# Pooled attention in front of a SiLU layer: the 72 keys of a head split into 64 and 8, in smaller array tiles

## The chip, the cores and the metric

The kernel runs on one core of one Trainium2 chip. The metric is the device time of one execution in microseconds (us). PE is the matmul engine, DVE the vector engine, ACT the scalar engine, POOL the GpSimd engine, and SP an engine that here only issues transfers.

## The reference

```python
k_p = k.reshape(B, H, 72, 8, D).mean(axis=3)        # B = 8, H = 8, S = 576, D = 64
v_p = v.reshape(B, H, 72, 8, D).mean(axis=3)
scores = np.matmul(q, k_p.transpose(0, 1, 3, 2)) / np.sqrt(D)
attn = np.exp(scores - max); attn = attn / (sum + 1e-09)
x = (attn @ v_p) -> [4608 tokens, 512]
h = x @ w_in                                        # [512, 2048]
out = (h * sigmoid(h)) @ w_out                      # [2048, 512]
```

Each query of a head sees 72 pooled keys. All heads of a token side by side make the 512 inputs of the layer behind.

## The kernel before, in words

**Tiles and steps.** The 4608 tokens are taken in NT = 9 tiles of 512 (a tile can hold tokens of two batches, since a batch has 576; in units of 32 tokens, tile t takes 2t units of batch t-1 and 16-2t of batch t). Tile 0's attention is made first, in a piece of its own. After that the loop over t makes the two products of the layer for tile t, and beside them, in the same queue of PE, the attention of tile a = t+1. The products are made with sums of blocks (seven products of half size in place of eight): `x_sum` and `w_sum` are sums of blocks of the input and the weights, `h_sum` of the hidden values. They are DVE's work (lines 479, 474, 579, 590).

An order written by hand, such as `FOUR` for t from 2 to 7 or `FIRST` for t = 0, gives the sequence of products. `a1 a5 b1 ...` are units of the first product (two steps each of two matmuls of 256 columns); `P1 Q1 ... P4 Q4` are the first and second half of products of the second (four steps of two matmuls each). `at(s, fn, ...)` and `late(s, fn, ...)` place other work behind step s. The order in each engine's queue is the order in which this code runs: no scheduler moves anything later. In `FOUR`, step 63 is the end of unit d4, in front of P2; steps 68 to 75 are P5 and Q5 (they load `h_sum0`), 76 to 83 P6 and Q6 (`h_sum1`), 84 to 87 Q2, 88 to 91 P7.

**Banks.** PSUM has eight banks here: three under the tag `mm` and five under the tag `at`. The products use `mm` for `u_psB`, `o_psA`, `o_psB` and `o_psE`, and `at` for `u_psA` and `u_psE`. Attention takes its banks from `at` for the most part. A new tile of a tag gets the bank that was given back first.

**Attention of one tile (a >= 1).** PE can be cut into smaller arrays ("lanes") that work beside each other, each on its own rows and columns. The tile is made in two halves of 256 queries (f = 0, 1), in three visits to PE:

- step 63, `scores(a, 0)` and step 78, `scores(a, 1)`: `score_matmuls` (line 331) multiplies `kz` (keys, transposed, 32 rows for half of a head's dimensions) by `qT`. Lanes of 32 rows and 128 columns; four heads s in four lanes, c = 0, 1 the two halves of the dimensions, g = 0, 1 the two groups of four heads. Results are four banks `sc_ps` of 72 keys x 512; ACT makes `es`, their exponentials (line 356).
- step 89, `denominators` (line 363, `ones` times `es`), `numerators` (line 378, `vp`, the pooled values, times `es`) for both halves. Lanes of 128 rows (72 used) and 32 columns, four at once. ACT makes logarithm and exponential of the denominators (lines 368 and 373: `lnd`, `rec`), and `x_half` (line 413, DVE) multiplies `nu_ps` by `rec` into `xT`, from which the `x_sum`s of the next tile are made.

**Keys and values.** For batches 3 and up POOL loads k and v in two halves that are added in transfer (`load_one`, `load_rest`), adds the rest up (`pool_rows`, lines 189 and 192), and PE transposes the keys (`k_transpose`, step 34), ACT copying them into `kz` (line 213). Batches 0 to 2 go another way: rows are summed (`slot_sums`, line 261: DVE, in part POOL) and PE picks the rows of each head (`select_k`, line 283; `select_v`, line 301), ACT copying the result (`copy_v`, line 308).

Of the kernel before, what the change touches and what calls it, by code (L numbers as in the profile page):

```python
# [36 lines left out]
def kernel(  # L37
# [62 lines left out]
    ones = singles.tile([SP, 32], BF16, name="ones")  # L100
# [18 lines left out]
    kz = [singles.tile([128, 2, 2, SP], BF16, name=f"kz{n}") for n in range(2)]  # L119
    kp = singles.tile([128, H, D], BF16, name="kp")  # L120
# [44 lines left out]
    PH = POOL // 2 * D  # L165

# [9 lines left out]
    def load_one(b, name):  # L176
        st = batches.setdefault(b, {})
        raw = raw_tile(f"{name}_raw3", H)
        nc.gpsimd.dma_start(out=raw, in_=source(b, name)[:, :, :PH])
        st[f"{name}_raw"] = raw  # L180

    def load_rest(b, name):
        nc.gpsimd.dma_start(
            out=batches[b][f"{name}_raw"], in_=source(b, name)[:, :, PH:],
            accum_op=ALU.add,
        )
# [9 lines left out]

    def pool_v(b):
        st = batches[b]
        st["vp"] = mid.tile([SP, H, D], BF16, tag="vp", name="vp")
        pool_rows(st["vp"], st["v_raw"])  # L200
# [91 lines left out]
    def select_v(b, a, tag="at"):  # L292
        st = batches[b]
        if a == 0:
            st["v_ps"] = ps_tile([128, H, D], FP32, tag, "v_ps")
            st["vp"] = mid.tile([SP, H, D], BF16, tag="vp", name="vp")
# [8 lines left out]

    def copy_v(b, a, copy=nc.vector.tensor_copy, heads=4):
        hs = slice(4 * a, 4 * a + heads)
        copy(out=batches[b]["vp"][:, hs, :], in_=batches[b]["v_ps"][:SP, hs, :])
# [14 lines left out]
    def es_tile():  # L323
        return mid.tile([SP, 4, 2 * NQ], BF16, tag="es", name="es")
# [25 lines left out]
    def scores(t, f):  # L350
        sc = [ps_tile([128, 512], FP32, "at", "sc_ps")[:SP] for s in range(4)]
        for g in range(2):
            score_matmuls(sc, t, f, g, g * NQ)
        es = half_state(t, f)["es"] = es_tile()
        for s in range(4):
            nc.scalar.activation(es[:, s, :], sc[s], func=AF.Exp, scale=score_scale)  # L356

    def denominators(t, f, den_ps=None):
# [3 lines left out]
        for s in range(4):  # L362
            nc.tensor.matmul(  # L363
                den_ps[32 * s : 32 * (s + 1), :],
                lhsT=ones, rhs=st["es"][:, s, :], start=True, stop=True,
# [9 lines left out]
    def numerator_matmuls(nu, t, f, g, c, c0):  # L375
        for b, _, cs in half_units(t, f):
            for s in range(4):
                nc.tensor.matmul(  # L378
                    nu[32 * s : 32 * (s + 1), c0 + cs.start : c0 + cs.stop],
                    lhsT=batches[b]["vp"][:, 4 * g + s, c::2],  # L380
# [20 lines left out]
    def numerators(t, f, tags=("at", "at")):  # L401
        st = half_state(t, f)
        nu = []
        for c in range(2):
            nu.append(ps_tile([128, 512], FP32, tags[c], "nu_ps"))
            for g in range(2):
                numerator_matmuls(nu[c], t, f, g, c, g * NQ)
        st["nu"] = nu

    def x_half(t, f):  # L410
        st = half_state(t, f)
        for c in range(2):
            nc.vector.tensor_mul(  # L413
                out=xT[:, c::2, x_cols(t, f)],
                in0=st["nu"][c].rearrange("r (g n) -> r g n", g=2),
                in1=st["rec"].rearrange("r (g n) -> r g n", g=2),
# [364 lines left out]
    nc.vector.memset(kp, 0.0)  # L781
    nc.gpsimd.memset(shifts, 0.0)
    make_identity(nc, ident, nomemset=True)

# [76 lines left out]
    for n in range(4):  # L861
        unit_weight_sum(0, 1, n)
    denominators(0, 1, den_ps)
# [28 lines left out]
    for t in range(NT):  # L892
        a = t + 1
        if t == 0:
# [17 lines left out]
            for j in range(2):  # L912
                at(60 + 2 * j, select_k, 1, j)
                at(60 + 2 * j, copy_k, 1, j, nc.scalar.copy)
            for i0, i1 in ((0, SA), (SA, SLOTS), (SLOTS, SLOTS + 1)):
# [9 lines left out]
            for j in range(2):  # L925
                at(83 + j, slot_sums, "v", j)
                at(100 + j, select_v, 1, j)
            at(101, copy_v, 1, 0, nc.scalar.copy, H)
# [5 lines left out]
            at(68, scores, 1, 0)  # L934
            at(79, scores, 1, 1)
            at(79, denominators, 1, 0)
            at(94, reciprocals, 1, 0)
            at(103, denominators, 1, 1)
            at(103, reciprocals, 1, 1)
            at(106, numerators, 1, 0)  # L940
            at(106, numerators, 1, 1, ("at", "mm"))
# [107 lines left out]
```

## Time and profile before

| | |
|---|---|
| median of 3 runs | 273.23 us (273.04 to 273.35) |
| span of the profiled execution (first to last instruction) | 272.3 us |
| median less that span | 0.9 us |
| mean granted clock of PE | 0.999 |
| busy: PE, DVE, ACT, POOL | 266.3, 206.5, 194.1, 102.3 us |

The profiled execution has no time of its own beside its span; the 0.9 us is what lies around the span in the median run. In a line of the timeline the columns are the start in us from the span's start, the length of the group in us, the engine, the line of the kernel, the operation, what is written and read, shape and number of instructions. Matmuls overlap, so a group's length reaches beyond the start of the next group. In `128*128` or `72*32` the first number is rows, the second columns of the array in use.

### The profile page before, as it was taken

The page shows a single profiled execution, that of the slowest core. Times are in us where ns is not written, and L with a number is a line of the kernel's source. Part 1 is how long each engine was busy: PE and PEld are TensorE (multiplying, and loading weights), DVE is VectorE, ACT ScalarE, POOL GpSimd, SP SyncE. Part 2 cuts the span into 40 slices and gives each one's busy share as a digit, 9 for nine tenths or more (in the row PEclk, how much of TensorE's full clock was granted, in tenths as well). Part 3 has the DMA queues.
Part 4 walks back from the last instruction along what each step waited for, and adds up shares of the span by engine and source line. Part 5 has one row for each costly group of instructions (what it writes and reads, how often), then busy time and mean ns, then how long its engine had stood idle before and what let it go on. Part 6 is the DMA issues. An engine that isn't in the chain of part 4 may idle for free.

```text
span 272.3 us, 7297 instructions
## 1 busy us (share of the span) xinstructions
PE 266.3 (98%) x2982; PEld 213.9 (79%) x2982; DVE 206.5 (76%) x363; ACT 194.1 (71%) x342; POOL 102.3 (38%) x111
## 2 busy tenths in 40 slices
PE   8999999999999999999999999999999999999994
PEld 4358644788888878887888788878888888788883
DVE  4759886879697949794979497849875987587861
ACT  1579776888858885888588858785878587867700
POOL 8655435672348413831383329383800000000000
PEclk9999999999999999999999999999999999999999
DMA  7999999586996796679657976799400140014004
GB/s 214 269 203 281 216 289 304 177 150 156 133 200 168 148 137 150 157 148 147 132 140 164 125 154 164 155 130 123 126 2 2 40 117 1 2 34 120 4 2 154
DMA packets 31585, 37.72 MB, mean 139 GB/s; under 512 B 10640, under 2 KB 22608, under 8 KB 31552
## 3 DMA queue, kind: packets, MB, share of 16 engines
q0 software_dynamic: 23904, 26.64, 52.4%
q1 hardware_dynamic: 7216, 9.97, 13.3%
q10 hardware_dynamic: 432, 0.66, 0.7%
q8 instruction: 23, 0.38, 0.6%
q14 instruction: 10, 0.08, 0.1%
HBM read 36.70 MB, written 9.44 MB: 169 GB/s over the span
## 4 chain that ended last, share of the span: by engine, by line
PE 92%; DMA 6%; POOL 0%; issue 0%; DVE 0%; POOLq 0%
PE u_psB L636 17%; PE o_psB L655 16%; PE u_psA L636 11%; PE u_psE L636 11%; PE o_psA L655 11%; PE o_psE L655 10%; PE o_ps L553 5%; PE sc_ps L331 3%; DMA raw<-in_v_dram 3%; DMA w_in_sb<-in_moe_w_in_dram 3%; PE nu_ps L378 3%; PE hp_ps L525 2%; PE den_ps L363 2%; POOL q_bf L127 0%; PE kz_ps L283 0%
## 5 line engine op out<-in xcount | busy, mean ns | idle before, releaser
L636 PEld LDWEIGHTS <-w_sum 128*128 128x128 bf16 x544 | 52.8, 98 | 7.5 <-issue 1.0
L655 PEld LDWEIGHTS <-h_sum 128*128 128x128 bf16 x512 | 48.6, 98 | 9.1 <-issue 2.6
L636 PEld LDWEIGHTS <-w_in_sb 128*128 128x128 bf16 x408 | 39.9, 98 | 5.0 <-issue 0.2
L655 PEld LDWEIGHTS <-h_T 128*128 128x128 bf16 x384 | 36.9, 98 | 5.3 <-issue 1.0
L636 PE MATMUL u_psA<-xT,w_in_sb 128*128 128x256 bf16 x272 | 40.5, 273 | 0.0
L636 PE MATMUL u_psB<-x_sum,w_sum 128*128 128x256 bf16 x272 | 40.2, 272 | 0.0
L356 ACT ACTIVATE es<-sc_ps 72x512 bf16<-72x512 f32 x64 | 32.7, 590 | 2.8 <-PE sc_ps L331 1.9
L655 PE MATMUL o_psB<-w_sum,h_sum 128*128 128x256 bf16 x256 | 33.0, 273 | 0.0
L655 PE MATMUL o_psA<-w_out_sb,h_T 128*128 128x256 bf16 x256 | 32.1, 273 | 0.0
L670 DVE TENSOR_TENSOR u_psE<-u_psB,p 128x512 f32<-128x512 f32 x34 | 23.7, 697 | 10.0 <-ACT p L668 6.1
L413 DVE TENSOR_TENSOR xT<-nu_ps,rec 128x512 bf16<-128x512 f32 x32 | 20.4, 683 | 12.6 <-ACT rec L373 10.5
L674 ACT ACTIVATE h_T<-u_psE 128x512 bf16<-128x512 f32 x34 | 20.3, 597 | 11.2 <-PE u_psE L636 10.4
L687 DVE TENSOR_TENSOR c<-u_psB,p 128x512 f32<-128x512 f32 x34 | 23.2, 681 | 3.1 <-PE u_psB L636 2.1
L665 DVE COPY u_psB<-u_psA 128x512 f32<-128x512 f32 x30 | 20.9, 698 | 5.5 <-PE u_psA L636 3.8
L674 ACT ACTIVATE h_T<-u_psB 128x512 bf16<-128x512 f32 x34 | 20.4, 599 | 5.9 <-PE u_psB L636 5.9
L674 ACT ACTIVATE h_T<-u_psA 128x512 bf16<-128x512 f32 x34 | 20.5, 602 | 4.7 <-PE u_psA L636 4.5
L189 POOL TENSOR_TENSOR raw<-raw 72x1024 f32<-72x1024 f32 x10 | 23.6, 2357 | 0.1
L668 ACT COPY p<-u_psE 128x512 f32<-128x512 f32 x34 | 20.0, 593 | 4.2 <-PE u_psE L636 4.0
L579 DVE TENSOR_TENSOR h_sum<-h_T 128x1024 bf16<-128x1024 bf16 x32 | 21.7, 680 | 0.2 <-ACT h_T L674 0.2
L674 ACT ACTIVATE h_T<-c 128x512 bf16<-128x512 f32 x34 | 21.7, 637 | 0.0
L579 DVE TENSOR_TENSOR h_sum<-h_T,h_sum 128x1024 bf16<-128x1024 bf16 (+1 forms) x24 | 20.7, 864 | 0.2
L636 PE MATMUL u_psB<-xT,w_sum 128*128 128x256 bf16 x136 | 20.6, 272 | 0.0
(89 smaller groups left out, 438.7 us busy)
## 6 DMA issues: line engine op xcount, KB each, us to landing
out_dram<-o_sb SPq DMA_DIRECT2D x128, 64.0 KB, 1.7
raw<-in_k_dram POOLq DMA_DIRECT2D x10, 576.0 KB, 8.2
raw<-in_v_dram POOLq DMA_DIRECT2D x10, 576.0 KB, 8.6
q_bf<-in_q_dram POOLq DMA_DIRECT2D x5, 576.0 KB, 11.3
w_in_sb<-in_moe_w_in_dram POOLq DMA_DIRECT2D x8, 256.0 KB, 8.6
w_out_sb<-in_moe_w_out_dram POOLq DMA_DIRECT2D x4, 512.0 KB, 10.7
raw<-in_v_dram POOLq DMA_DIRECT2D x2, 768.0 KB, 10.4
raw<-in_k_dram POOLq DMA_DIRECT2D x2, 768.0 KB, 10.0
```

Source lines behind the costliest of these rows:

```text
L189: nc.gpsimd.tensor_add(out=raw[:, :, : 2 * D], in0=raw[:, :, : 2 * D], in1=raw[:, :, 2 * D :])
L356: nc.scalar.activation(es[:, s, :], sc[s], func=AF.Exp, scale=score_scale)
L413: nc.vector.tensor_mul(out=xT[:, c::2, x_cols(t, f)], in0=st["nu"][c].rearrange("r (g n) -> r g n", g=2), in1=st["rec"].rearrange("r (g n) ...
L553: nc.tensor.matmul(ps["m", m], lhsT=h_T[:, g, m * 128 : (m + 1) * 128], rhs=w_out_sb[:, g, :], start=(g == 0), stop=(g == KG - 1),)
L579: nc.vector.tensor_tensor(out=h_sum[n][:, k0:k1, :], in0=get(a), in1=get(b), op=op)
L636: nc.tensor.matmul(ps[y, BANK[n]][:, u, :], lhsT=w[:, kk, 128 * u : 128 * (u + 1)], rhs=x[:, kk, :], start=n in (1, 5) and u == 0 and kk == 0,
L655: nc.tensor.matmul(o_bank(n, c), lhsT=left(n, kt, c), rhs=w[:, kt, :], start=n in (1, 5) and kt == 0 and c == 0, stop=kt == KQ - 1, skip_g ...
L665: (acopy if t == 0 or (t == 1 and y in (0, 1)) else vcopy)(ps[y, "B"], ps[y, "A"])
L668: acopy(f32[y], ps[y, "E"])
L670: tt(out=ps[y, "E"], in0=ps[y, "B"], in1=f32[y], op=add)
L674: nc.scalar.activation(h_T[:, g : g + 2, j * NQ : (j + 1) * NQ], src, func=AF.Silu)
L687: tt(out=c22, in0=ps[y, "B"], in1=f32[y], op=add)
```

## The change

From tile 1 on a head's 72 keys are held as 64 and 8. The 64 keys of two heads (g = 0, 1) lie one above the other on 128 partitions, the 8 keys of four heads on 32. A tile is made whole (512 queries, no halves) in two visits.

- `scores(t)`: 64 keys in lanes of 32 rows x 64 columns (eight lanes: four s, two g); then the 8 keys of four heads at once in lanes of 128 x 32, with `kzr`, a copy of the keys that is zero outside a head's own rows. `spread_keys` makes it on DVE with one multiplication by `mask_k`, behind ACT's copy of the keys. ACT makes `es` (128 x 512, four) and `er` (128 x 256, one).
- `sum_matmuls(t)` and `value_matmuls(t)`: lanes of 64 x 32 for the 64 keys and for the sums; lanes of 32 x 128 for the 8 keys' values, with `vr`, made from the values by `spread_values` with `mask_v` (two multiplications; POOL, or DVE for batches 1 and 2). There are two `den_ps` banks and four `nu_ps` banks, the fourth from `mm`.
- Values: `pick_v` in place of `select_v` for batches 1 and 2, and for batch 0 a second time for tile 1; for later batches `load_one` and `load_half` bring 64 keys of v on 128 partitions (POOL) and the 8 keys with four transfers on SP, and `pool_v` adds them up.
- The masks are made at the start. The visits stand at steps 63 and 88 (t >= 1), and at 70, 87 and 106 in t = 0; `slot_sums` of v in t = 1 goes from step 69 to 62.

```diff
+    def scores(t):
+        st = att[t] = {}
+        sc = [ps_tile([128, 512], FP32, "at", "sc_ps") for _ in range(4)]
+        scr = ps_tile([128, 512], FP32, "at", "sr_ps")
+        for n, (b, us, cs) in enumerate(tile_units(t)):
+            for c in range(2):
+                for s in range(4):
+                    rows = slice(32 * s, 32 * (s + 1))
+                    for g in range(2):
+                        nc.tensor.matmul(
+                            sc[s][KM * g : KM * (g + 1), cs],
+                            lhsT=kz[b % 2][rows, g, c, :KM],
+                            rhs=qT[rows, g, us, :, c],
...
+                nc.tensor.matmul(
+                    scr[32 * n : 32 * (n + 1), cs],
+                    lhsT=kzr[b % 2][:, g, c, :], rhs=qT[:, g, us, :, c],
...
+    def sum_matmuls(t):
...
+        lanes = [(s, g, slice(KM * g, KM * (g + 1))) for s in range(4) for g in range(2)]
+        for s, g, rows in lanes:
+            one(s, g, slice(0, NTT), ones[rows], st["es"][rows, s, :], start=True, stop=False)
+        for f in range(2):
+            cols = slice(f * NQ, (f + 1) * NQ)
+            for s, g, rows in lanes:
+                one(s, g, cols, ones_r[rows, 4 * f + s], st["er"][rows], start=False, stop=True)
...
+    def value_matmuls(t, tags=("at", "at", "at", "mm")):
...
+        for f in range(2):
+            for c in range(2):
+                for n, (b, _, cs) in enumerate(half_units(t, f)):
+                    for s in range(4):
+                        for g in range(2):
+                            rows = slice(KM * g, KM * (g + 1))
+                            nc.tensor.matmul(
+                                nu[g][f][32 * s : 32 * (s + 1), c, cs],
+                                lhsT=batches[b]["vp"][rows, s, c::2],
+                                rhs=st["es"][rows, s, f * NQ + cs.start : f * NQ + cs.stop],
...
+                nc.tensor.matmul(
+                    nu[g][f][:, c, cs],
+                    lhsT=batches[b]["vr"][rows, c].rearrange("r s d -> r (s d)"),
+                    rhs=st["er"][rows, cs], start=False, stop=True, skip_group_check=True,
+                )
...
+    def x_part(t, g):
+        st = att[t]
+        inv = st["inv"][g].rearrange("r (f n) -> r f n", f=2)
+        for f in range(2):
             nc.vector.tensor_mul(
+                out=xT[:, 2 * g : 2 * g + 2, x_cols(t, f)], in0=st["nu"][g][f],
+                in1=inv[:, f : f + 1, :].broadcast_to([128, 2, NQ]),
...
+    def spread_keys(b, eng=nc.vector):
+        eng.tensor_tensor(
+            out=kzr[b % 2].rearrange("r a c (s k) -> r (a c) s k", s=4),
...
+            in1=mask_k.unsqueeze(1).unsqueeze(3).broadcast_to([128, 4, 4, SP - KM]),
+            op=ALU.mult,
...
+    def pick_v(b):
...
+                    nc.tensor.matmul(
+                        ps[KM * g : KM * (g + 1), s, :], lhsT=shifts[:, x : x + KM],
+                        rhs=v5[:, i], start=(s == 0 and j == 0), stop=(j == len(segs) - 1),
...
+        for n in range(4):
+            for s in range(4):
+                h = 4 * (n // 2) + s
+                nc.tensor.matmul(
+                    ps[32 * n : 32 * (n + 1), 4, :], lhsT=pick_r[:, h],
+                    rhs=v5[:, (SP * h + KM) // 128], start=False, stop=(s == 3),
...
+        nc.scalar.copy(value_tile(b), ps)
...
+            at(47, spread_keys, 0)
+            at(59, pick_v, 0)
+            at(60, spread_values, 0)
+            at(63, spread_keys, 1)
...
-            at(101, copy_v, 1, 0, nc.scalar.copy, H)
+            at(100, pick_v, 1)
+            at(101, spread_values, 1, nc.vector)
...
-            at(68, scores, 1, 0)
-            at(79, scores, 1, 1)
-            at(79, denominators, 1, 0)
-            at(94, reciprocals, 1, 0)
-            at(103, denominators, 1, 1)
-            at(103, reciprocals, 1, 1)
-            at(106, numerators, 1, 0)
-            at(106, numerators, 1, 1, ("at", "mm"))
-            for n in range(2):
-                at(106, x_half, 1, n)
+            at(70, scores, 1)
+            at(87, sums, 1)
+            at(106, value_matmuls, 1)
+            for g in range(2):
+                at(106, x_part, 1, g)
...
-                    at(69, slot_sums, "v", j, halves=True)
+                    at(62, slot_sums, "v", j, halves=True)
...
-                for j in range(2):
-                    at(84, select_v, 2, j)
-                at(84, copy_v, 2, 0, nc.scalar.copy, H)
+                at(32, spread_keys, 2)
+                at(76, pick_v, 2)
+                at(77, spread_values, 2, nc.vector)
...
+                at(35, spread_keys, a)
...
-            late(63, scores, a, 0)
-            late(78, scores, a, 1)
-            late(89, denominators, a, 0)
-            late(89, reciprocals, a, 0)
-            late(89, denominators, a, 1)
-            late(89, reciprocals, a, 1)
-            for n in range(2):
-                late(89, numerators, a, n)
-            late(89, x_half, a, 0)
-            late(91, moe_tables)
-            late(95, x_half, a, 1)
+            late(63, scores, a)
+            late(88, sums_and_values, a)
+            late(89, x_part, a, 0)
+            late(89, moe_tables)
+            late(95, x_part, a, 1)
```

## The prediction

> **What bounds the kernel now.** I read the page first (shares of the engines, the chain of waits), then the timeline of PE over one steady tile (t=3, 105 to 133 us), then the timelines of DVE and ACT where attention hands work over.
>
> ```profile
> PE 266.3 (98%) x2982; PEld 213.9 (79%) x2982; DVE 206.5 (76%) x363; ACT 194.1 (71%) x342; POOL 102.3 (38%) x111
> ...
> PE 92%; DMA 6%; POOL 0%; issue 0%; DVE 0%; POOLq 0%
> ```
>
> PE has work through the whole span and carries 92% of the chain. So only what lengthens or shortens PE's own queue counts; other engines count where PE would have to wait for them. PE's timeline in tile 3 (start, length, line, matmuls):
>
> ```profile
> 118.93 0.60 PE L636 MATMUL u_psB<-xT,w_sum 128*128 128x256 bf16 x4
> 119.46 0.65 PE L331 MATMUL sc_ps<-qT,kz 32*72 32x256 bf16 x16
> 120.04 1.05 PE L655 MATMUL o_psA<-w_out_sb,h_T 128*128 128x256 bf16 x8
> ...
> 126.13 0.60 PE L655 MATMUL o_psB<-w_sum,h_sum 128*128 128x256 bf16 x4
> 126.66 0.62 PE L363 MATMUL den_ps<-es,ones 72*32 72x512 bf16 x8
> 127.10 1.06 PE L378 MATMUL nu_ps<-es,vp 72*32 72x256 bf16 x32
> 128.09 1.49 PE L655 MATMUL o_psB<-w_sum,h_sum 128*128 128x256 bf16 x12
> ```
>
> A full-array matmul of 256 columns takes 0.109 (12 from 128.09 to 129.41). A visit costs its start to start less the full ones in it. First scores: 120.04 - 118.93 - 4 x 0.109 = 0.67. Second scores (122.67 to 124.00, six full ones): 0.68. Third visit: 128.09 - 126.13 - 4 x 0.109 = 1.52. Sum 2.87 a tile. Inside them four lanes run at once: eight waves of `nu` take 8 x 0.109 and 0.12 to get back to the full array; a `den` wave of 512 columns takes 0.22 (126.66 to 127.10, two); getting in costs 0.09 (126.66 less 126.57); lanes cut by rows need 0.03 more for the first wave (0.58 = 4 x 0.109 + 0.12 + 0.03). From one lane shape to another:
>
> ```profile
> 38.71 0.65 PE L331 MATMUL sc_ps<-qT,kz 32*72 32x256 bf16 x16
> 39.29 0.40 PE L363 MATMUL den_ps<-es,ones 72*32 72x512 bf16 x4
> ```
>
> the same 0.58, so a direct switch costs about 0.10.
>
> **Steady tiles, t=2 to 7.** The new scores: 64 keys in 32x64 lanes, eight at once, two waves of 512 columns (0.44); 8 keys in 128x32 lanes, two waves of 256 (0.22); in, first wave, switch, out: 0.09 + 0.03 + 0.10 + 0.12 less rounding. Together 0.98. The new second visit: sums 0.22 + 2 x 0.109, values 4 x 0.109, rest values 2 x 0.109, and the same overheads: 1.42. Sum 2.40, 0.47 less than 2.87; six tiles give -2.8.
>
> Eight lanes at once is not in this trace. The nearest rows are four lanes that share all rows (`den`, `nu`) and four that share all columns (`sc`); both run fully beside each other, and a lane in the new shapes shares its rows with at most three others, as in `den`. I take full speed, and price the other end below.
>
> What else these tiles need. ACT makes 4 exps and a short one instead of 8 (590 ns each): less, and ACT is not what PE waits for. The 8-key exp ends before P5's copy of `o_psE` is due. DVE gets `spread_keys`, 128 bf16 elements: between 0.09 (memset of 72x32) and 0.42 (`x_sum`, 512 elements), nearest 0.2; it waits for ACT's `kz` copy (113.67 to 114.09) and stands where DVE sits idle for 0.84 until 115.09, so it costs nothing; behind it in DVE's queue is the `u_psE` add of unit d, which was waiting for ACT longer. POOL adds half as many elements of v (72x1024 took 2.36) plus three short adds and two masked copies, about the same 3.6 in all; two more DMA issues (L179 0.9, L183 1.4) put q's load 2.3 later, which lands at 133.7 and is wanted at 138.5. SP's four loads of the 8 keys wait for POOL's adds early in the tile; behind them on SP stand stores due 15 us later. The reciprocals: counted back from the tile's end, Ln can start 0.27 after the last `den` wave, 5.7 us before the end (5.8 before: 127.11 to 132.91), and four products of 0.6 follow as before; the first `x_sum`, which had 0.9 to spare (132.44 against 133.34), keeps 0.8.
>
> **Tile 0.** Before, its visits cost 0.71 + 1.01 + 0.35 (`select_v`) + 0.43 + 1.10 = 3.60. After: `pick_v` twice, scores 0.98, sums alone 0.65, values alone 0.99. `pick_v` is 12 matmuls of 128x64 in two lanes and 16 of 128x32 in four: with `v_ps`'s 29 ns (12 in 0.35, 69.82 to 70.17) a round it is 0.09 + 6 x 0.029 + 0.10 + 4 x 0.029 + 0.12 = 0.60; with no lanes beside each other 28 x 0.029 + 0.31 = 1.12. I take 0.65, near the lower end because lanes do run together above.
> [...] No row here loads 64 columns.
> PE's own sum is 3.93, +0.33. Then the hand-over into tile 1, from the timelines of PE and DVE:
>
> ```profile
> 47.34 2.12 PE L553 MATMUL o_ps<-w_out_sb,h_T 128*128 128x512 bf16 x9
> ...
> 50.34 1.03 PE L636 MATMUL u_psE<-x_sum,w_sum 128*128 128x256 bf16 x8
> ```
>
> ```profile
> 46.87 2.48 DVE L413 TENSOR_TENSOR xT<-nu_ps,rec 128x512 bf16<-128x512 f32 x4 [2.03 <-PE nu_ps L378]
> 49.27 0.68 DVE L561 COPY o_sb<-o_ps 128x512 f32<-128x512 f32 x1
> 49.87 0.75 DVE L479 TENSOR_TENSOR x_sum<-xT 128x512 bf16<-128x512 bf16 x2
> ```
>
> The first `x_sum` is done at 49.87 + 0.42 = 50.29 and PE uses it at 50.34: no slack. Before, the products began at 46.87 while PE was still at the second half's values. Now no bank is complete until the last rest wave. The visit starts at 46.24 + 0.44 = 46.68, that wave 0.66 to 0.77 later, and a matmul lasts 0.27: products from 47.75, 0.88 later, and `u_psE` 0.88 later with them. **Tile 0 costs +0.88**, of which 0.55 is waiting.
>
> **Tile 1.** `slot_sums` of v moves from step 69 to 62, in front of the `h_sum`s in DVE's queue:
>
> ```profile
> 64.31 0.68 DVE L579 TENSOR_TENSOR h_sum<-h_T 128x1024 bf16<-128x1024 bf16 x1
> ...
> 66.71 0.55 DVE L261 TENSOR_TENSOR raw<-raw 128x384 f32<-128x384 f32 x1
> 67.29 0.36 DVE L261 TENSOR_TENSOR v<-raw 128x192 bf16<-128x192 f32 x1
> 67.57 0.42 DVE L261 TENSOR_TENSOR raw<-raw 128x256 f32<-128x256 f32 x1
> 68.02 0.29 DVE L261 TENSOR_TENSOR v<-raw 128x128 bf16<-128x128 f32 x1
> 68.23 1.22 DVE L579 TENSOR_TENSOR h_sum<-h_T,h_sum 128x2048 bf16<-128x2048 bf16 x1
> ```
>
> ```profile
> 65.43 1.91 PE L655 MATMUL o_psE<-w_sum,h_sum 128*128 128x256 bf16 x16
> ```
>
> They take 68.23 - 66.71 = 1.52. The first `h_sum0` half then ends at 64.31 + 1.52 + 0.68 = 66.51; PE reaches P5, which loads it, at 65.43 + 0.31 = 65.74: a wait of 0.77. P5 lasts 0.87, to 67.38; the second half (65.50 to 66.19 before) ends at 67.71: 0.33 more. Further: scores +0.31, second scores -0.68, `pick_v` for `select_v` +0.30, last visit -0.10. **Tile 1: +0.93.**
>
> At the start the masks cost nothing: DVE's memsets lie in its 2.39 us wait for `raw` of k, its ten mask operations in the 2.83 us before 20.22, and POOL's three (0.3 each) ahead of DMA issues that wait 2.29 for other landings; uncovered, up to 0.7.
>
> **Sum.** 0.88 + 0.93 - 2.8 = -1.0. The span is 272.3, the median of the runs 273.23; the 0.9 around the span stays. 273.23 - 1.0 = **272.2**.
>
> **Rivals.**
> *Lanes that share rows take turns* (slower). For it: no row has the array cut both ways. Against it: four lanes on the same rows run beside each other in `den`. Every eight-lane wave then counts twice: scores 0.44, sums 0.44, values 0.44, 1.3 a tile; eight tiles 10.5: 282.7. It decides from the point where an eight-lane wave takes 1.1 times the time of one matmul in it (0.13 a tile eats the -1.0). Chance 0.10.
> *Starts are too slow for eight lanes.* Eight matmuls must start within 109 ns. The `kz` selection (24 matmuls of 128x32, 56.32 to 56.65, a way out of 0.1 in it) shows one in 10 ns or less: 80 ns, hidden save in waves of 64 columns, 0.1 in two tiles. If a start needed the 29 ns of `v_ps`, a wave of 256 would take 0.23 and the six of them 0.74 more a tile: 278.1 over eight tiles. Chance 0.02.
> [...]
> *A new wait in every second visit* (no change, or a little slower). The fourth `nu` bank is an `mm` bank, that of `o_psA`, and waits for DVE's copy into `o_sb` (L700). Before, that copy began 0.31 after the start of Q2's last matmul (126.18 against 125.11 + 7 x 0.109) and took 0.69: it ends at 1.00. From the same start PE wants the bank at 0.11 + 0.22 (one step of P7) + 0.09 + 0.44 + 0.22 = 1.08. Were DVE 0.25 late, 0.17 in each of seven tiles would be lost, 273.4; 0.4 late, 274.5. For it speaks the small slack, against it that DVE had ended the add ahead of that copy (125.38, 0.70) before PE let the copy go. Chance 0.22.
> *Neither wait in tiles 0 and 1 appears*: -1.0 - 0.55 - 1.1, 270.6. Against it stand the two orders above. Chance 0.12.
>
> **How the numbers follow.** The forecast has 0.54, its own range 271.4 to 273.0 (`pick_v` up to 1.12, 0.03 more or less per switch over 40 switches). The range 270.4 to 275.0 reaches over the no-wait case and the new wait, and leaves out the lanes. Runs of this kernel differ by 0.1%, so 0.2% (0.55 us) is what a measurement can tell: faster means under 272.68. Of the forecast 0.72, of the third rival 0.05 and all of the fourth lie there: 0.52. Slower: the lanes and slow starts 0.12, half of the third rival, a little of the forecast: 0.26. Same: 0.22.
>
> **What would show it.** Per steady tile the two visits should cost 0.98 and 1.42 on PE; eight `sc` matmuls should start within 0.05, and an `nu` wave take 0.109. PE's idle or start gaps should appear at `u_psE` of tile 1 (0.55, behind `x_sum`) and at P5 and Q5 of tile 1 (0.77, 0.33, behind `h_sum`), and nowhere else. Waves of 0.2 in place of 0.109, or a gap in front of the `nu` of g=1, f=1, would prove me wrong.

## The result, and the profile after

| | median | runs | ratio to before |
|---|---|---|---|
| kernel before | 273.27 us (273.04 to 274.0) | 9 | |
| changed kernel | 274.76 us (274.05 to 276.38) | 9 | 1.0059 (1.0037 to 1.008) |

The change makes the kernel 1.5 us slower; forecast was 1.0 us faster. The profiled execution of the changed kernel has a span of 274.2 us; the nine spans reach from 272.3 to 274.5, and every time is its span plus 1.7 to 2.0. In a later set of six runs of the same kernel the spans were 272.4 to 273.3 (e13 below), where those of the kernel before were 271.2 to 272.4. So the change costs 1.0 at least, and in some executions 1.4 to 1.8 more (that is how much longer tile 0 is in the first profile and in that of e1 than in that of e13). The page of the changed kernel, shares of the engines and the chain that ended last:

```profile
PE 264.4 (96%) x3228; PEld 212.9 (78%) x3234; DVE 214.3 (78%) x392; ACT 180.5 (66%) x319; POOL 113.1 (41%) x151
...
PE 86%; DVE 5%; ACT 1%; issue 1%; DVEq 0%
```

PE is busy 1.9 us less than before, as it was meant to be, and yet its share of the chain fell from 92% to 86%: DVE now carries 5%. PE waits for DVE, where before it did not. PE's longest waits behind the start (us in total, times, longest; PE's warm-up at the start waits 1.3, and 1.2 in the kernel before):

```profile
PE nu_ps L573 <- DVE vr L248: 1.0, 1, 1.0
PE u_psB L824 <- DVE u_psB L853: 0.7, 1, 0.7
PE o_psE L843 <- ACT es L528: 0.6, 1, 0.6
PE u_psE L824 <- DVE x_sum L667: 0.6, 1, 0.6
```

All four lie between 47 and 71 us, in tiles 0 and 1. The fourth was forecast, the third too (as a wait for `h_sum0`; the name that the line gives is a wrong one, see e4). The first two were not. First the steady tile, for the visits themselves; PE's timeline in tile 3:

```profile
123.20 0.60 PE L824 MATMUL u_psB<-xT,w_sum 128*128 128x256 bf16 x4
123.73 0.66 PE L507 MATMUL sc_ps<-qT,kz 32*64 32x256 bf16 x32
124.33 0.41 PE L520 MATMUL sr_ps<-qT,kzr 128*32 128x256 bf16 x8
124.67 1.05 PE L843 MATMUL o_psA<-w_out_sb,h_T 128*128 128x256 bf16 x8
...
130.07 0.38 PE L843 MATMUL o_psB<-w_sum,h_sum 128*128 128x256 bf16 x2
130.38 0.41 PE L536 MATMUL den_ps<-es,ones 64*32 64x512 bf16 x8
130.61 0.40 PE L536 MATMUL den_ps<-er,ones_r 64*32 64x256 bf16 x16
130.83 0.62 PE L561 MATMUL nu_ps<-es,vp 64*32 64x256 bf16 x32
131.38 0.40 PE L573 MATMUL nu_ps<-er,vr 32*128 32x256 bf16 x8
131.71 1.70 PE L843 MATMUL o_psB<-w_sum,h_sum 128*128 128x256 bf16 x14
```

The 32 value matmuls are four waves (a wave is one matmul in each lane, all at once) of eight lanes; they take 131.38 - 130.83 = 0.55, which is 4 x 0.109 and one switch of 0.11. So eight lanes do run beside each other at full speed, 0.109 a wave as for one matmul of the full array. The scores cost 124.67 - 123.20 - 4 x 0.109 = 1.03, the second visit 131.71 - 130.07 - 2 x 0.109 = 1.42 (forecast 0.98 and 1.42). No gap stands in front of the fourth `nu` bank.

Tile 0, where the loss begins (timeline of all engines, lines of DVE, POOL and PE):

```profile
45.45 3.07 POOL L323 TENSOR_TENSOR raw<-raw 128x768 f32<-128x768 f32 x2 [0.94 <-DMA raw<-in_k_dram]
45.83 2.85 DVE L248 TENSOR_TENSOR vr<-vp,mask_v 128x128 bf16<-128x128 bf16 x2 [0.93 <-ACT vp L394]
...
48.73 0.28 PE L573 MATMUL nu_ps<-er,vr 32*128 32x256 bf16 x5 [0.98 <-DVE vr L248]
...
51.47 0.68 DVE L749 COPY o_sb<-o_ps 128x512 f32<-128x512 f32 x1
52.07 0.75 DVE L667 TENSOR_TENSOR x_sum<-xT 128x512 bf16<-128x512 bf16 x2
52.54 0.72 PE L824 MATMUL u_psE<-x_sum,w_sum 128*128 128x256 bf16 x5 [0.60 <-DVE x_sum L667]
```

The two multiplications that make `vr` for the rest values take 2.85 us here; the same two take 0.49 in tile 1 (at 73.59). PE starts nothing in the middle of the rest values from 47.57 to 48.73. Beside them, from 45.45 on, POOL makes two long additions. Behind that comes the forecast wait for `x_sum`.

Tile 1 (DVE's timeline):

```profile
58.06 0.70 DVE L853 COPY u_psB<-u_psA 128x512 f32<-128x512 f32 x1 [0.47 <-PE u_psA L824]
60.59 0.29 DVE L256 TENSOR_TENSOR kzr<-kz,mask_k 128x128 bf16<-128x128 bf16 x1 [1.83 <-ACT kz L352]
60.80 0.30 DVE L165 STREAM_TRANSPOSE qT<-q_bf 128x128 f32<-128x128 f32 x1
61.03 0.67 DVE L853 COPY u_psB<-u_psA 128x512 f32<-128x512 f32 x1
...
67.59 0.55 DVE L323 TENSOR_TENSOR raw<-raw 128x384 f32<-128x384 f32 x1
68.17 0.36 DVE L323 TENSOR_TENSOR v<-raw 128x192 bf16<-128x192 f32 x1
68.45 0.42 DVE L323 TENSOR_TENSOR raw<-raw 128x256 f32<-128x256 f32 x1
68.90 0.29 DVE L323 TENSOR_TENSOR v<-raw 128x128 bf16<-128x128 f32 x1
69.11 0.68 DVE L767 TENSOR_TENSOR h_sum<-h_T 128x1024 bf16<-128x1024 bf16 x1
```

DVE sat idle 1.83 us in front of `kzr`, a product of 0.29 us that PE needs only at 67.8, because ACT reaches its copy of `kz` late; the copy of `u_psA` that PE waits for is queued behind it. That could be read in the profile of before, where DVE copies `u_psA` before ACT has made `kz`:

```profile
57.58 0.70 DVE L665 COPY u_psB<-u_psA 128x512 f32<-128x512 f32 x1 [0.83 <-ACT h_T L674]
57.86 0.48 ACT L290 CAST kz<-kz_ps 128x144 bf16<-128x144 f32 x2
```

In the timeline of the changed kernel, further down, `slot_sums` of v stands ahead of `h_sum`, as forecast.

What each stage cost, from the same products of PE in three profiles (first `u_psE` product of tile 0 to that of tile 1; from there to P5 of tile 1; then P5 to P5 of the next tile):

| | before | after, first profile | after, profile of e13 |
|---|---|---|---|
| tile 0 | 26.16 | 28.91 | 27.52 |
| tile 1 up to P5 | 15.09 | 17.31 | 17.31 |
| P5 of tile 1 to P5 of tile 2 | 27.86 | 28.37 | 28.37 |
| five steady tiles, mean | 27.64 | 27.31 | 27.25 |

The steady tiles gain; tiles 0 and 1 lose 5.5 us in the first profile and 4.1 in the other (0.34 of it is the first scores of tile 2, which fall into the third row). In tile 0 the two profiles differ in `vr` alone: in e13 it took 0.49 us (45.68 to 46.17), and POOL's additions began after it, at 46.90. The lines of e13:

```profile
45.68 0.49 DVE L248 TENSOR_TENSOR vr<-vp,mask_v 128x128 bf16<-128x128 bf16 x2
46.90 3.03 POOL L323 TENSOR_TENSOR raw<-raw 128x768 f32<-128x768 f32 x2 [1.74 <-DMA raw<-in_k_dram]
```

The 0.06 between their steady tiles is one pause of 0.3 in the first profile, at 185.67.

### The profile page after: what moved, and what is told of

Read it like the earlier page. It is cut to its first block, busy times and chain, and to the rows that moved or that the text cites. A ratio compares the mean times of both kernels' runs of the same rounds, so it can differ in the third digit from the quotient of the medians.

```text
span 274.2 us, 7884 instructions
## 1 busy us (share of the span) xinstructions
PE 264.4 (96%) x3228; PEld 212.9 (78%) x3234; DVE 214.3 (78%) x392; ACT 180.5 (66%) x319; POOL 113.1 (41%) x151
## 4 chain that ended last, share of the span: by engine, by line
PE 86%; DVE 5%; ACT 1%; issue 1%; DVEq 0%
PE o_psB L843 16%; PE u_psB L824 16%; PE u_psE L824 10%; PE o_psA L843 10%; PE o_psE L843 10%; PE u_psA L824 10%; PE o_ps L741 4%; PE hp_ps L713 2%; PE den_ps L536 2%; PE sc_ps L507 2%; PE nu_ps L561 1%; DVE vr L248 1%; PE nu_ps L573 1%; DVE xT L602 1%; PE sr_ps L520 1%; ACT h_T L862 1%
## 5 line engine op out<-in xcount | busy, mean ns | idle before, releaser
L843 PEld LDWEIGHTS <-h_sum 128*128 128x128 bf16 x512 | 49.2, 98 | 9.1 <-DVE h_sum L767 1.6
L843 PEld LDWEIGHTS <-h_T 128*128 128x128 bf16 x384 | 37.0, 98 | 5.2 <-issue 0.4
L843 PE MATMUL o_psA<-w_out_sb,h_T 128*128 128x256 bf16 x256 | 31.9, 273 | 0.0
L843 PE MATMUL o_psB<-w_sum,h_sum 128*128 128x256 bf16 x256 | 31.9, 273 | 0.0
L584 ACT ACTIVATE lnd<-den_ps 128x512 f32<-128x512 f32 x16 | 9.6, 597 | 20.5 <-PE den_ps L536 20.3
L767 DVE TENSOR_TENSOR h_sum<-h_T 128x1024 bf16<-128x1024 bf16 x32 | 21.7, 681 | 0.2 <-ACT h_T L862 0.2
L202 POOL DMA_DIRECT2D v_raw<-in_v_dram x20 | 18.2, 1016 | 8.3 <-DMA v_raw<-in_v_dram 8.3
L767 DVE TENSOR_TENSOR h_sum<-h_T,h_sum 128x1024 bf16<-128x1024 bf16 (+1 forms) x24 | 20.8, 865 | 0.3
L824 PE MATMUL u_psE<-x_sum,w_sum 128*128 128x256 bf16 x136 | 20.3, 273 | 0.6 <-DVE x_sum L667 0.6
```

Of the source, the lines that this page charges most:

```text
L202: nc.gpsimd.dma_start(out=batches[b]["v_raw"][KM * g : KM * (g + 1)], in_=source(b, "v")[:KM, 4 * g : 4 * (g + 1), PH * half : PH * (half ...
L584: nc.scalar.activation(ln, st["den"][g], func=AF.Ln)
L767: nc.vector.tensor_tensor(out=h_sum[n][:, k0:k1, :], in0=get(a), in1=get(b), op=op)
L824: nc.tensor.matmul(ps[y, BANK[n]][:, u, :], lhsT=w[:, kk, 128 * u : 128 * (u + 1)], rhs=x[:, kk, :], start=n in (1, 5) and u == 0 and kk == 0,
L843: nc.tensor.matmul(o_bank(n, c), lhsT=left(n, kt, c), rhs=w[:, kt, :], start=n in (1, 5) and kt == 0 and c == 0, stop=kt == KQ - 1, skip_g ...
```

## The experiments

All times are medians of 6 to 12 executions; "before" is the kernel before on the same chip. e7 and e8 are one execution each, made for their profiles (274.71 and 274.74 us).

| run | this | before | ratio |
|---|---|---|---|
| e1, keys of tile 1 later | 274.19 | 273.2 | 1.0034 (1.0013 to 1.0054) |
| e2, POOL behind `vr` | 274.28 | 273.2 | 1.0036 (1.0023 to 1.0048) |
| e3, `vr` from PSUM | 274.65 | 273.2 | 1.0046 (1.0031 to 1.0062) |
| e4, sums of v later | 273.56 | 273.2 | 1.0021 (1.0002 to 1.0039) |
| e6, four edits | 272.52 | 273.42 | 0.9958 (0.9942 to 0.9973) |
| e9, and values earlier | 273.45 | 273.42 | 1.0003 (0.9987 to 1.002) |
| e10, copy on ACT | 272.58 | 273.21 | 0.9971 (0.996 to 0.9983) |
| e11, and values earlier | 271.94 | 273.21 | 0.9958 (0.9942 to 0.9974) |
| e12, mended | 271.54 | 273.19 | 0.994 (0.9924 to 0.9956) |
| e13, the change again | 274.41 | 273.19 | 1.0046 (1.0028 to 1.0063) |

**e1: the masked keys of tile 1 later in DVE's queue.**

```diff
-                at(32, spread_keys, 2)
+                at(50, spread_keys, 2)
```

> The changed kernel with one edit: in tile 1 the masked 8 keys (spread_keys) are made by DVE at step 50 in place of step 32. Theory A (the queue): in the changed kernel DVE sat idle 1.83 us in front of this operation, waiting for ACT's kz copy, with the copy of u_psA into u_psB queued behind it, and PE waited 0.91 and 0.15 us for that copy. Then both waits vanish and the time falls by about 1.06, from 274.76 to 273.7; the h_sum waits (0.79 and 0.32) stay. Theory B (ACT itself is late there, and DVE's queue only shows it): the copy of u_psA or the u_psE adds then wait for ACT in the same place, PE's gap stays at 0.7 or more, and the time at 274.7.

DVE's timeline of e1, the same stretch:

```profile
58.99 0.30 DVE L165 STREAM_TRANSPOSE qT<-q_bf 128x128 f32<-128x128 f32 x1
60.12 0.70 DVE L853 COPY u_psB<-u_psA 128x512 f32<-128x512 f32 x1 [0.83 <-ACT h_T L862]
60.73 0.69 DVE L858 TENSOR_TENSOR u_psE<-u_psB,p 128x512 f32<-128x512 f32 x1
```

The copy starts as soon as its own inputs allow, and both gaps of PE in front of `u_psB` (0.91 and 0.15) are gone: theory A. From the first `u_psE` product of tile 1 to P5 it is 16.25, where the change has 17.31: 1.06 less. The median fell by only 0.6, because the twelve spans stand in two groups, six at 271.2 to 271.7 and six at 273.0 to 273.5. The profiled execution is of the upper one, and in it `vr` took 3.22 us for the two. The lower group lies 1.0 under the lowest spans of the changed kernel (272.3 to 272.6), which fits the 1.06.

**e2: POOL's additions held behind `vr`.** A copy of one column on POOL that reads `vr` now stands ahead of the additions.

```diff
+            at(102, lambda: nc.gpsimd.tensor_copy(out=gate, in_=batches[1]["vr"][:, 1, 3, 31:]))
-                at(93, slot_sums, "k", j, levels=(0,), eng=nc.gpsimd)
+                at(103 + j, slot_sums, "k", j, levels=(0,), eng=nc.gpsimd)
```

> The changed kernel with one edit: in tile 0 POOL's two long adds of k (3.07 us) are held back behind DVE's masked values vr by a small POOL copy that reads vr; nothing is left out. Theory A (POOL and DVE block each other on SBUF): the two vr operations, 1.27 and 1.58 us beside POOL's adds, take about 0.28 each as in tile 1, the gaps of 1.16 and 0.26 in front of the rest values vanish, and the time falls by 1.2 to 1.5, to 273.3 to 273.6. Theory B (vr is slow there for a reason of its own): 2.85 us for the two as before, and 274.8. POOL's adds then run from about 46.5 to 49.6 and still end ahead of the 53.8 at which POOL's next work starts.

The operations of line 248 on DVE, count and shortest, median and longest in ns; first in the changed kernel, then in e2:

```profile
L248 DVE TENSOR_TENSOR vr<-vp,mask_v x4: 284/819/1582, 45.8 to 73.8; 128x128 bf16<-128x128 bf16 x4
```

```profile
L248 DVE TENSOR_TENSOR vr<-vp,mask_v x4: 285/288/293, 45.9 to 72.4; 128x128 bf16<-128x128 bf16 x4
```

Theory A for the operation: with POOL's additions held back all four take 0.285 to 0.293. The spans of e2's eight runs are 272.1 to 272.9, one group. The time, 274.28, misses the 273.3 to 273.6 expected: that sum took the whole gap off the median, but not every execution of the changed kernel had a gap to lose (in the profile of e13 `vr` took 0.49).

**e3: `vr` from PSUM.** DVE reads the bank `v_ps` in place of ACT's copy of it.

```diff
+        st["v_rest"] = ps[:, 4]
-        rest = st["vp"][:, 4].rearrange("r (p c) -> r c p", c=2)
+        rest = st.get("v_rest", st["vp"][:, 4]).rearrange("r (p c) -> r c p", c=2)
-            at(60, spread_values, 0)
+            at(60, spread_values, 0, nc.vector)
```

> The changed kernel with one edit: the masked values vr of batches 0, 1 and 2 are made by DVE from the PSUM bank v_ps in place of ACT's copy of it in SBUF, so that one of the two inputs of the operation lies in SBUF and DVE need not wait for ACT. Theory A (it is the second SBUF input that POOL's adds block): vr takes 0.3 to 0.45 each beside POOL's adds, starts 0.4 earlier, the gaps of 1.16 and 0.26 vanish, 273.3 to 273.6. Theory B (POOL's adds slow any DVE operation): vr stays at 1.2 or more each, and the time falls by the 0.4 of the earlier start alone, to 274.4.

`vr` took 0.49 for the two and no gap was left, but in this execution it started at 45.65 and POOL's additions at 46.00, so that neither theory was tested; the earlier start did not come either (1.28 behind the start of `pick_v`, as before). Six spans, 272.3 to 273.1. Inconclusive; e7 and e8 force the meeting, and in e6 and e10 it came about by itself: POOL's addition was under way (from 45.18 and 45.41) when `vr` from PSUM began (45.47 and 45.63), and the two took 0.49.

**e7 and e8: POOL made to add at that moment.** Both have three more POOL additions; `vr` comes from SBUF in e7 and from PSUM in e8.

```diff
+            for n in range(3):
+                at(92, lambda: nc.gpsimd.tensor_add(
+                    out=warm.rearrange("r (a n) -> r a n", a=4), in0=warm32.unsqueeze(1).broadcast_to([128, 4, 128]),
+                    in1=warm32.unsqueeze(1).broadcast_to([128, 4, 128])))
```

> The changed kernel with three more POOL additions in tile 0 (two inputs in SBUF, 512 elements, onto a tile that nothing reads any more), placed so that POOL is adding at the moment at which DVE makes vr; nothing is left out. Theory A (POOL's read and an operation of DVE with two inputs in SBUF exclude each other): vr, from SBUF here, takes over 0.8 us each in place of 0.28, PE has gaps in front of the rest values. Theory B: 0.28 each.

> The same three POOL additions, with vr made from the PSUM bank v_ps. Theory A (only the second SBUF input is blocked): 0.28 each although POOL adds beside it, and no gap in front of the rest values. Theory B (POOL's additions slow every operation of DVE): as long as from SBUF.

The timeline of DVE and POOL, e7:

```profile
43.84 1.93 DVE L778 TENSOR_TENSOR w_sum<-w_out_sb,w_sum 128x1024 bf16<-128x1024 bf16 x1
44.17 3.76 POOL L1144 TENSOR_TENSOR warm<-warm 128x512 bf16<-128x512 f32 x3
45.70 1.32 DVE L248 TENSOR_TENSOR vr<-vp,mask_v 128x128 bf16<-128x128 bf16 x2
```

and e8:

```profile
43.93 2.06 DVE L779 TENSOR_TENSOR w_sum<-w_out_sb,w_sum 128x1024 bf16<-128x1024 bf16 x1
44.38 3.63 POOL L1145 TENSOR_TENSOR warm<-warm 128x512 bf16<-128x512 f32 x3
45.92 0.49 DVE L248 TENSOR_TENSOR vr<-v_ps,mask_v 128x128 bf16<-128x128 f32 x2
```

In e8 POOL adds through the whole of `vr` and `vr` takes 0.49, as if alone. In e7 the first of the two took 1.12, from 45.70 to 46.82, and ended 0.15 behind POOL's second addition (46.67); the second took 0.28 and started 0.006 ahead of POOL's third. (Theory A had over 0.8 for each; that holds for the first. It also had gaps of PE in front of the rest values: they lost 0.2 at most. PE waited for `x_sum` instead, 1.13 against 0.77 in e13; the first `x_sum`, both inputs in SBUF, took 0.78 beside POOL's last addition, 0.42 in e13.) In the first profile of the change the two, of 1.58 and 1.35, also end 0.15 behind the end of the addition beside them (47.41 and 48.68 against 47.25 and 48.53). In e7 and e8 the `w_sum` in front, with two inputs in SBUF, takes 1.93 and 2.06 where its neighbours take 0.68. Theory A. The first profile says the same over the whole run: DVE's sums from PSUM (`u_psE`, `c`) take 0.68 to 0.70 beside POOL's additions and products (33 times), no longer than alone (0.65 to 0.70); `kzr`, both inputs in SBUF, takes 0.25 to 0.29 alone and 0.48 to 0.62 in four of the five times beside them. The fifth time, 0.28, it had begun 0.05 ahead of POOL.

In these runs it counted where the inputs lay: the two `vr` with both inputs in SBUF took 1.32 beside POOL's additions (e7), with one of the two in PSUM 0.49 (e8). For `vr` it counted too which of the engines began first: from SBUF the two took 0.49 where they began 0.27 ahead of POOL's additions (e4, 45.60 against 45.87; POOL's two took 3.12 there, 3.03 in e13), and 2.85 where POOL began 0.38 ahead of them (first profile, 45.45 against 45.83). The `w_sum`s of e7 and e8 do not follow that order: by the profile they started 0.33 and 0.45 ahead of POOL's additions and took 1.93 and 2.06 all the same; why stays open.

**e4: `slot_sums` of v behind the `h_sum`s again.**

```diff
-                    at(62, slot_sums, "v", j, halves=True)
+                    at(69, slot_sums, "v", j, halves=True)
-                at(76, pick_v, 2)
-                at(77, spread_values, 2, nc.vector)
+                at(79, pick_v, 2)
+                at(80, spread_values, 2, nc.vector)
```

> The changed kernel with slot_sums of v in tile 1 at step 69 again (62 in the change), behind the h_sums in DVE's queue, and pick_v and vr of tile 1 at steps 79 and 80 in place of 76 and 77. Theory A (as predicted): PE's waits of 0.79 at P5 and 0.32 at Q5 of tile 1 vanish, 1.1 less, 273.6. Theory B: the wait at P5 is for the first exp of the scores, which the profile names there (ACT es, 0.6 us), and DVE's order is not what counts: 0.6 to 0.8 stays at P5, only the 0.32 goes, 274.4. If pick_v or vr at the later step comes too late, a new gap shows in front of v_ps or of the rest values.

PE's waits at P5 and Q5 (0.79 and 0.32) are both gone. P5 in e4, and the first exp of the scores, from the timelines of PE and ACT:

```profile
66.54 1.05 PE L843 MATMUL o_psA<-w_out_sb,h_T 128*128 128x256 bf16 x8
67.43 1.91 PE L843 MATMUL o_psE<-w_sum,h_sum 128*128 128x256 bf16 x16
```

```profile
67.62 2.06 ACT L528 ACTIVATE es<-sc_ps 128x512 bf16<-128x512 f32 x4
```

P5 starts 0.19 before the exp does, so it does not wait for it. In the changed kernel the line "o_psE <- ACT es" named the exp only because it ended there (69.26 + 0.60) next to the `h_sum` (69.11 + 0.68). Theory A. Eight of the twelve spans are 271.1 to 272.2, four 272.9 to 273.4.

**e6: these edits together, and the first two `x_sum`s ahead of DVE's copy of `o_ps`.** The edits of e1, e3 and e4, and:

```diff
-            for n in (0, 2, 1, 3):
-                at(0, unit_x_sum, 1, n)
+            for n in (1, 3):
+                at(0, unit_x_sum, 1, n)
...
+            for n in (0, 2):
+                at(106, unit_x_sum, 1, n)
```

> The changed kernel with four edits together: keys of tile 1 masked at step 50, vr of batches 0 to 2 from PSUM, slot_sums of v in tile 1 behind the h_sums (with pick_v and vr at 79 and 80), and in the hand-over of tile 0 the first two x_sums ahead of DVE's copy of o_ps into o_sb. Theory A (three separate waits on DVE, which add up): the runs of the changed kernel without the blocked vr stand at 274.1; less 1.06, 1.11 and about 0.5 of the 0.77 in front of u_psE gives 271.4, about 1.8 under the kernel before, in one group of runs. Theory B (the waits hide one another: PE meets the next late operation instead, ACT's exps at P5 or the adds in tile 1): at most half of it, 272.7 to 273.2.

272.52 lies between the two theories. The upper group is gone (seven spans, 269.9 to 271.0), but 1.1 of theory A's forecast is missing. By the stages the waits do add up: tiles 0 and 1 (up to P5 of tile 2) are 2.30 shorter than in e13, where 2.67 was forecast, and the profiled execution took 271.64; the rest of the median's 1.1 does not show in the stages of its profile. In the hand-over the 0.77 in front of `u_psE` became 0.30 there and 0.39 in front of `u_psB`, where PE now waits for the third `x_sum` behind the copy. That edit brought 0.08, not 0.5. The start of an execution varies by over a microsecond of its own (the first `u_psE` product stands at 23.46 in e13, 24.18 in the profile of before and 24.54 in e12).

**e9: the values of tile 1 earlier.**

```diff
-            at(100, pick_v, 1)
-            at(101, spread_values, 1, nc.vector)
+            at(96, pick_v, 1)
+            at(97, spread_values, 1, nc.vector)
...
-            at(106, value_matmuls, 1)
+            at(103, value_matmuls, 1)
```

> The same four edits, and in tile 0 pick_v and vr at steps 96 and 97 (100, 101), the values and the x products at 103 (106). Theory A (the hand-over of tile 0 is set by the time at which the rest values end): the x products start 0.65 earlier, the rest of the wait in front of u_psE (0.2 to 0.3) goes, 271.1. Theory B (DVE is full there: three sums of w_out, 1.9 us, stand behind vr and ahead of the products): the x products start no earlier, PE's gap stays, 271.4 or slower.

Theory B, and worse than expected, for the reason found in e7: a sum of DVE with two inputs in SBUF meets POOL's addition. DVE and POOL in e9:

```profile
45.83 3.85 POOL L323 TENSOR_TENSOR raw<-raw 128x768 f32<-128x768 f32 x2 [1.61 <-DMA raw<-in_k_dram]
```

```profile
46.25 2.30 DVE L779 TENSOR_TENSOR w_sum<-w_out_sb,w_sum 128x1024 bf16<-128x1024 bf16 x1
48.47 2.47 DVE L603 TENSOR_TENSOR xT<-nu_ps,rec 128x512 bf16<-128x512 f32 x4
```

One `w_sum` of 0.68 took 2.30 (and POOL's two additions 3.85, 3.07 in the first profile), and the x products behind it started at 48.47 where the rest values were done near 47.

**e10 and e11: the copy of `o_ps` of m=1 on ACT; then the values earlier, with the `w_sum`s ahead of `vr`.** Here m counts the four blocks of 128 tokens of tile 0's output. Both have the edits of e1, e3 and e4, and:

```diff
-            copy = nc.vector.tensor_copy if m == 1 else nc.scalar.copy
-            copy(o_sb[m // 2][:, m % 2, :], ps["m", m])
+            nc.scalar.copy(o_sb[m // 2][:, m % 2, :], ps["m", m])
...
-            at(107, moe_tables)
+            at(102, moe_tables)
```

> The changed kernel with the keys at step 50, vr from PSUM, the sums of v behind the h_sums, and the hand-over of tile 0 eased in another way: the copy of o_ps of m=1 into o_sb is made by ACT in place of DVE (and ACT's table is loaded at step 102, 107 before), so that nothing stands between the x products and the four x_sums on DVE. Theory A (in the run with the four edits the copy stood behind two x_sums and PE waited 0.30 in front of u_psE and 0.39 in front of u_psB, the latter for the third x_sum): the 0.39 goes, the 0.30 stays, 0.4 less than with the four edits, about 272.1. Theory B (the second copy of u_psA into u_psB on ACT takes the place of the x_sum as the last to come): the 0.39 stays in front of u_psB, 272.5.

> The same, and in tile 0 pick_v and vr at 96 and 97, the values and x products at 103, the three sums of w_out at 95 in place of 99 (so that they stand ahead of vr, where DVE is idle, and not between vr and the products beside POOL's additions, where one of them took 2.30 us), and the masked keys of batch 0 at 50 in place of 47. Theory A: the x products start 0.65 earlier and PE's last wait at the hand-over (0.30) goes, and 0.13 in front of u_psB in tile 0: 271.7. Theory B (the products then wait for another engine, or a bank of the values is not free at 103): PE's gap in front of u_psE or of the values stays, 272.1 or more.

The wait in front of `u_psB` went (A), but 272.58 and 271.94 are 0.5 and 0.2 above the numbers of theory A. PE in e10:

```profile
46.40 0.50 PE L562 MATMUL nu_ps<-es,vp 64*32 64x64 bf16 x33
47.54 0.41 PE L562 MATMUL nu_ps<-es,vp 64*32 64x256 bf16 x15 [0.64 <-ACT o_sb L749]
```

The table load of 1.28, moved to 102, stands ahead of ACT's copy of m=0, which starts 1.07 later than in the first profile of the change (both counted from the first `u_psE` product); that copy frees the fourth `nu` bank. It is the third rival of the prediction, in tile 0, made by the experiment.

**e12: the table load behind that copy, the values at 104.** As e11, with

```diff
-            at(107, moe_tables)
+            at(104, moe_tables)
...
+            at(104, value_matmuls, 1)
```

> The kernel with the values at 103, mended: ACT's table is loaded at step 104, behind its copy of o_ps of m=0, and the values and x products of tile 1 stand at 104. Theory A (in the two runs before, the table load of 1.28 us stood ahead of the copy that frees the fourth bank of the values, and PE waited 0.67 and 0.46 us for it in the middle of the values; it is the wait for a bank that the prediction had as a rival for the steady tiles, in tile 0): this wait goes, none comes in front of u_psE, 0.4 to 0.5 less than 271.94, about 271.5, all runs in one group. Theory B (the load now delays the copy of m=1 or of m=2, and these the copies of u_psA): a new gap in front of u_psA or u_psB, 271.9 or more.

271.54, 0.6% under the kernel before, and the fastest of all. In tiles 0 and 1 no wait of PE over 0.21 us is left; five of six spans are 269.4 to 269.7. Theory A. The chain of e12:

```profile
PE 91%; DMA 6%; issue 1%; POOL 0%; DVE 0%; DVEq 0%; POOLq 0%
```

DVE has left it; that is the chain of before.

**e13: the change again.**

> The changed kernel once more, unedited, on the same chip as the mended one. Theory A (vr against POOL's additions is a race that POOL's landing decides anew in each run): spans in groups, the lowest at 272.3 and another 1.2 to 1.9 above it. Theory B (one fixed time): spans within 0.8 us of each other, as those of the kernel with POOL held back (272.1 to 272.9).

By the spans (272.4 to 273.3, 0.1 more than its 0.8) theory B; no run of this set fell into an upper group. POOL's additions started at 46.90 here, when `vr` was done, and at 45.45 in the first profile. That `vr` from SBUF is slow where POOL's addition is under way at its start is shown by the first profile (2.85 for the two) and e7 (1.12 for the first), and that it is not where it comes first by e2, e4 and this profile (0.49 for the two in each); that the upper groups of spans are the executions in which POOL came first is seen in the few that were profiled, and not shown for the others. How many spans stand high differs from set to set (three of nine at 274.2 or more in the first, none of six here), and the sets did not all run on one chip; why POOL's additions start at 45.45 in one profile and at 46.90 in the other, each time behind the landing of k (`DMA raw<-in_k_dram`), stays open.

## Why the prediction was wrong

**The visits: right in the main.** Full speed in eight lanes (0.109 a wave), 1.42 for the second visit where a tile lies within one batch. The scores cost 1.03, not 0.98. Where a tile's queries belong to two batches the waves are cut into pieces of 64, 128 or 192 columns and the second visit takes longer: in tile 2 it is 104.50 - 102.74 - 2 x 0.109 = 1.54. The prediction gave 0.1 in two tiles for that; in e13 the six second visits came to 1.55, 1.42, 1.52, 1.49, 1.46 and 1.42. The steady tile gained 0.39 (e13) in place of 0.47.

**The first step that failed: "`spread_keys` ... costs nothing".** That was worked out in a steady tile, where the operation stands behind a copy of ACT that is early. In tile 1 the keys come by another way (`select_k` at 30, ACT's copies at 31), and `spread_keys` stands at 32, ahead of DVE's copy of `u_psA`. The prediction never went there. The question of what is queued behind a waiting instruction was asked for the steady tiles alone. In place of nothing, PE waited 1.06 in tile 1, shown by e1.

**The second: "products from 47.75".** That took `vr` as ready when PE reached the last waves. Its two multiplications were priced nowhere in tile 0, and that POOL's additions lie on the same microseconds was in the profile of before:

```profile
46.24 3.05 POOL L261 TENSOR_TENSOR raw<-raw 128x768 f32<-128x768 f32 x2 [1.64 <-DMA raw<-in_k_dram]
```

With `vr` free the step is still 0.48 short: tile 0 cost +1.36 where 0.88 was forecast. The difference is in the main a wait for `x_sum` of 0.77 in place of 0.55, two `pick_v` of 0.75 in place of 0.65, and 0.13 behind `spread_keys` of batch 0, which also stood in front of a DVE sum that PE was waiting for (gone in e11, where it stands at 50). With `vr` blocked it cost +2.75.

**`pick_v`.** It cost 0.75 a time, not 0.65: PE's timeline of e2 has 45.26 - 44.60 + 0.09 = 0.75. The 0.65 was the author's estimate from the 29 ns a round of `v_ps`, whose matmuls load 128 columns; the rows of before load 128, 72 and 32 columns, and none 64. In e2 the twelve matmuls of 64 columns took 44.99 - 44.60 = 0.39 where six rounds of 29 ns and a switch of 0.10 give 0.27, and the sixteen of 32 columns with the way out 45.26 - 44.99 = 0.27 where the same rate gives 0.24.

**The waits at P5 and Q5: right to 0.02.** Forecast 0.77 and 0.33, measured 0.79 and 0.32, gone in e4. But the sum of tile 1 was +0.93 where +2.4 was measured (17.31 - 15.09 + 28.37 - 27.86, less the 0.34 of the next tile's scores). The 1.4 between them: the two waits behind `kzr` 1.06, the last visit 0.13, `pick_v` 0.10, a gap at 75.2 of 0.08, the scores 0.05.

**The sum.** In the forecast's terms it is +1.36 + 2.4 - 0.39 x 6 = +1.4 where `vr` is not blocked, against -1.0. Measured whole, from the first `u_psE` product of tile 0 to the end, e13 takes 0.8 more than before (248.9 against 248.1): some 0.3 was gained in tile 8 and 0.2 behind its P5, which no term of the forecast has and no run explains. The spans without a blocked `vr` say +1.0 (272.4 against 271.4). Some 0.5 more stands in the median of the first set; of its executions the profiled one had `vr` blocked, and for the others it is not shown. What "lies around the span" was 1.8 and not 0.9: the forecast set the span of one execution of before, 272.3, beside the time of another, and the usual span is 271.4 to 271.6. That shifted no difference. That 274.76 lies within the range of 270.4 to 275.0 is luck: its upper part was there for a wait in the second visits, which did not come.

**The rivals.** Lanes that take turns and slow starts fell: in tile 3 of the first profile a wave of eight takes 0.109, and most of its starts stand 3 to 4 ns apart. The wait for the fourth `nu` bank did not come in the change (no gap at the values of any steady tile but one at 185.67 that e13 does not have) and came in e10, when a step moved past ACT's copy. The case that happened, a DVE queue blocked by the change's own small products in tiles 0 and 1, was in none of the rivals: they spoke of the lanes, of a bank in the second visits, or took waits away.

## What to carry to other kernels

A small operation is priced by where it stands and not by its length: for every place at which it is issued, one asks what it waits for, what is queued behind it, and what the neighbouring engine does in the same microsecond. Prologue and first tiles use other code paths than the steady loop, and need their own walk through each queue. Here the new tiling gained 0.39 us in each steady tile, and the kernel became 0.6% faster than before once DVE's and ACT's queues in tiles 0 and 1 had been put in order (e12).

## What the runs showed that was not expected

- DVE's operations with both inputs in SBUF took longer beside POOL's additions: one `vr` 0.28 to 0.29 alone, 1.58 and 1.35 in the first profile, a `w_sum` of 0.68 up to 2.30 (e9). With one input in PSUM two `vr` took 0.49 beside POOL's additions (e6, e8, e10), as alone (e12). POOL's additions started behind the landing of k, 0.38 ahead of `vr` in the first profile and 1.22 behind its start in e13. The spans of e1 fall into two groups 1.8 us apart (middles 271.4 and 273.2); the one that was profiled, of the upper group, has `vr` blocked (3.22 for the two).
- A wait that the profile puts down to one engine can be another's: "o_psE <- ACT es" was DVE's `h_sum`, and the row of the weight load had it right (`PEld L843 <- DVE h_sum L767`, longest 0.9).
- In tile 3 of the first profile matmuls in eight lanes mostly start 3 to 4 ns apart and take 0.109 a wave of 256 columns (`nu_ps`, 130.83 to 131.38); a change of lane shape cost 0.09 to 0.11 in its second visit, three of them (in 130.38 - 130.07 - 2 x 0.109 = 0.09, to the rest values 0.11, out 131.71 - 131.38 - 2 x 0.109 = 0.11).
